# Splitting the first weight matrix out of the key refills of a decode kernel, and reordering its last loads and products

## The chip, the cores and the metric

The kernel runs on one core of a Trainium2 chip. The metric is the device time of one launch in microseconds. The core has a matrix engine (PE, with a separate row PEld for its weight loads), a vector engine (DVE), a scalar engine (ACT), a general engine (POOL) and a sync engine (SP), each with its own instruction stream. They are ordered against each other only by semaphores. Loads from memory are done by 16 DMA engines that work through queues. Nearly all loads of this kernel are issued by SP, so they stand in one queue, in the order in which SP issues them.

## The reference

For two rows `x` of 512 numbers, an attention over a cached window and a two-layer network are computed and mixed by a gate:

```python
q = (x @ wq)                                  # 32 heads of 128, in 8 groups of 4
k = k_cache[:, :, Sk - W:, :]                 # W = 4096 keys for each of 2 x 8 groups
v = v_cache[:, :, Sk - W:, :]
p = softmax(q k^T * Dh ** -0.5)               # 4 heads share one group of keys
a = (p v).reshape(B, Sq, Hq * Dh) @ wo
h = x @ w1 + b1                               # 512 -> 1792
b = (h * tanh(softplus(h))) @ w2              # 1792 -> 512
g = sigmoid((x * gate_w).sum(-1))
out = g * a + (1 - g) * b
```

All numbers are float32. Keys and values of the window are 33.5 MB each, `wq` and `wo` 8.4 MB each, `w1` and `w2` 3.7 MB each. Every byte is used once.

## The kernel before, in words

The work runs in eight turns, one for each group of keys (`HKV`), in a loop on each engine. The last turn differs a little, so several loops have seven passes (`PAIRS`) and a written-out eighth. There is one buffer for keys, `kslot`, and one for values, `vslot`.

`kslot` holds, for each of 128 partitions, 4 KB of `w1` (`w1s`, two of the fourteen 128-column blocks of `w1`), 32 KB of keys (`ks`) and 8 KB of the query weights of the next turn (`wqs`). One load fills it in each turn but the last. `vslot` holds 32 KB of values (`vs`), 4 KB of `w2` (`w2s`) and 8 KB of `wo` (`wos`), both of the turn before. The load of the first turn brings values alone, since nothing stood before it; the load of the seventh is split (values, then the rest: lines 124 and 127). In the last turn keys and values come in three pieces each, and behind them the `w2` and `wo` of the seventh turn and then the `wo` of the eighth (`wol`, three pieces).

What a turn does on each engine:

- **DVE** (`head`, lines 316 to 347) waits for the key load (`ld_k`). It makes the dot products of `x` with the four 512-wide halves of `w1s` (4 instructions, `hx`) and with the next turn's query weights (8 instructions, `queries`, `q8`); all of these stand at line 282. When PE has finished the scores it reduces their maximum (line 322), then writes the next queries into `qz` (line 291, `queries_out`). After the exponential it transposes the probabilities (line 330), forms the reciprocal of their sum and the factor `mkr`, waits for POOL's denominator (`hd`) and inverts it (line 339), waits for PE's product (`sD`), scales and reduces it (lines 342 and 345), and stores the attention output of the turn as weights for PE (`wst`, line 347).
- **PE** makes the scores (line 229) as soon as keys and queries are there, a few small products, the product of probabilities and values (line 240, signal `sD`), the products with `w2` (line 247) and `wo` (line 253) of the turn before, which go into one accumulator `acc` (signal `sP`), and the sum over the parts of the attention output (line 258).
- **ACT** takes the exponentials: that of the activation function (line 210), then that of the scores (line 212).
- **POOL** computes the activation function from `hx` (lines 184 to 201) and hands it to PE as `hst` (signal `hs`), one turn ahead of its use.

The order of the work around the change is set by SP's stream (lines 110 to 139). The key load of a turn waits for `qz` of the turn before, that is for the last use of `kslot` by DVE and PE. The value load waits for `sP` of the turn before (for `sD` alone in turns seven and eight, where only values are overwritten). SP works in order: a load behind a wait is issued when the wait is over.

At the end (lines 260 to 276, `last`) the accumulator is copied to `accs`, folded over its four row blocks by a product with `fold`, and the four blocks of the last `wo` are multiplied with `wst`. Two halves of the partitions of `fin` take these products: the upper half (`s = 1`) first `fold` and blocks 0 and 1, the lower half (`s = 0`) blocks 2 and 3. ACT copies the upper half to `fs` after the first signal `pe` (line 218), DVE adds it to the lower half after the second (line 354), and SP stores the result (line 358).

Of the kernel before, what the change touches and what calls it, by code (L numbers as in the profile page):

```python
# [4 lines left out]
AF = mybir.ActivationFunctionType  # L5
# [3 lines left out]
P = 128  # L9
B = 2  # L10
# [13 lines left out]
PAIRS = FC // 2  # L24
CHUNK = 8192
W1P = 2 * D
WQH = REP * D
SCALE = DH ** -0.5
BIG = 3.0e38
S = 16  # L30
# [2 lines left out]
NP = PAIRS - 1  # L33


def decode_kernel(nc, xg, wq0, kw, k7a, k7b, k7c, v0, vw, v6, ww5, v7a, v7b, v7c, w26, wo6, wo7a, wo7b, wo7c, out):
    T, V, A, G, SP = nc.tensor, nc.vector, nc.scalar, nc.gpsimd, nc.sync

    def sb(name, n, p=P):
        return nc.alloc_sbuf_tensor(name, [p, n], F32).ap()  # L40

    def ps(name, n):
        return nc.alloc_psum_tensor(name, [P, n], F32).ap()

    kslot = sb("kslot", W1P + CHUNK + WQH)
    w1s, ks, wqs = kslot[:, :W1P], kslot[:, W1P : W1P + CHUNK], kslot[:, W1P + CHUNK :]
    vslot = sb("vslot", CHUNK + 2 * D + WQH + S)
    vs, w2s, wos = vslot[:, :CHUNK], vslot[:, CHUNK : CHUNK + 2 * D], vslot[:, CHUNK + 2 * D : CHUNK + 2 * D + WQH]
    b1 = vslot[:, CHUNK + 2 * D + WQH : CHUNK + 2 * D + WQH + FC]
# [5 lines left out]
    b16, qz, wst, hst = (zeros[:, sum(widths[:i]) : sum(widths[: i + 1])] for i in range(len(widths)))  # L55
# [4 lines left out]
    fold = sb("fold", Q)  # L60
# [10 lines left out]
    q8 = sb("q8", B * REP)  # L71
    mx = sb("mx", 1)
    bias = sb("bias", 1)
    prob = sb("prob", 512)
    lsum = sb("lsum", 1)
    pT = sb("pT", 512)
    rcp = sb("rcp", 1)
    mkr = sb("mkr", BN)
    osc = sb("osc", BN * DH)
    osel = sb("osel", DH)  # L80
    junkw = sb("junk", 12 * D + P)
    junk = [junkw[:, j * D : j * D + D] for j in range(12)]
    hx = sb("hx", 4)
    hb = sb("hb", 4)
    pq = sb("pq", 8)
    mt = sb("mt", 4)
    mn = sb("mn", 4)
    md = sb("md", 4)
    mr = sb("mr", 4)
    accs = sb("accs", D)  # L90
    fs = sb("fs", 256, 64)
    res = sb("res", 256, 64)

    acc = ps("acc", D)
    sc = ps("sc", 512)
# [4 lines left out]
    lp = small[:, 0:1]  # L100
    ol = small[:, 8:16]

    names = ("ld_x ld_q ld_k ld_kb ld_kc ld_v ld_vb ld_vc ld_h ld_o ld_w0 ld_w1 ld_w2 c_id c_m c_z c_xb c_eg c_g c_mg "
             "gx g0 g1 g2 g3 g4 g5 hs vx q8 rcp os0 qz mx sA sB bias ex pT sC osel sD sP sE wst pq mkr hx hq hd hr accs pe fs res st").split()
    sem = {n: nc.alloc_semaphore(n) for n in names}


# [5 lines left out]
    for i in range(HKV):  # L113
        if i:
            SP.wait_ge(sem["qz"], S * (i + 1))
        if i < PAIRS:
            SP.dma_start(kslot, kw[i]).then_inc(sem["ld_k"], 16)
        else:
            for n, (f, t), src in zip(("ld_k", "ld_kb", "ld_kc"), parts, (k7a, k7b, k7c)):
                SP.dma_start(ks[:, f:t], src).then_inc(sem[n], 16)  # L120
        if i in (0, NP):
            if i:
                SP.wait_ge(sem["sD"], S * i)
            SP.dma_start(vs, (v0, v6)[i // NP]).then_inc(sem["ld_v"], 16)
            if i:
                SP.wait_ge(sem["sP"], S * i)
                SP.dma_start(vslot[:, CHUNK : CHUNK + 2 * D + WQH], ww5).then_inc(sem["ld_h"], 16)
        elif i < NP:
            SP.wait_ge(sem["sP"], S * i)
            SP.dma_start(vslot[:, : CHUNK + 2 * D + WQH], vw[i - 1]).then_inc(sem["ld_v"], 16)  # L130
        else:
            SP.wait_ge(sem["sD"], S * i)
            for n, (f, t), src in zip(("ld_v", "ld_vb", "ld_vc"), parts, (v7a, v7b, v7c)):
                SP.dma_start(vs[:, f:t], src).then_inc(sem[n], 16)
    SP.wait_ge(sem["sP"], S * PAIRS)
    SP.dma_start(w2s, w26).then_inc(sem["ld_h"], 16)
    SP.dma_start(wos, wo6).then_inc(sem["ld_o"], 16)
    for n, (f, t), src in zip(("ld_w0", "ld_w1", "ld_w2"), ((0, 2), (2, 3), (3, 4)), (wo7a, wo7b, wo7c)):
        SP.dma_start(wol[:, f * D : t * D], src).then_inc(sem[n], 16)
# [24 lines left out]
    for n in range(NH):  # L164
        i = G.tensor_copy(same.rearrange("p (j y n h) -> p j y n h", j=NJ, n=NH, h=REP)[:, :, :, n, :],
                          key.rearrange("p (y h) -> p y h", h=REP)[:, None].to_broadcast([P, NJ, 4, REP]))
# [39 lines left out]
    A.wait_ge(sem["c_eg"], 1)  # L206
    A.activation(eg, zg, AF.Exp, scale=-1.0).then_inc(sem["c_eg"], 1)
    with A.Fori(S, S * PAIRS + 1, S) as r:
        A.wait_ge(sem["pq"], r)
        A.activation(pq, pq, AF.Exp).then_inc(sem["hq"], S)  # L210
        A.wait_ge(sem["bias"], r)
        A.activation(prob, sc, AF.Exp, bias=bias, scale=SCALE, accum_out=lsum).then_inc(sem["ex"], S)  # L212
    A.wait_ge(sem["bias"], S * HKV)
    A.activation(prob, sc, AF.Exp, bias=bias, scale=SCALE, accum_out=lsum).then_inc(sem["ex"], S)
    A.wait_ge(sem["sP"], S * HKV)
# [6 lines left out]
    with T.Fori(S, S * (HKV) + 1, S) as r:  # L222
# [4 lines left out]
        for m in range(BN):  # L227
            for j in range(NJ):
                i = T.matmul(sc[Q * j : Q * j + Q, :], qz[:, m * Q : m * Q + Q],  # L229
                             ks[:, (m * NJ + j) * 512 : (m * NJ + j + 1) * 512],  # L230
                             start=(m == 0), stop=(m == BN - 1))
# [6 lines left out]
        for c in range(NC):  # L238
            j = c % NJ
            i = T.matmul(o[Q * j : Q * j + Q, :], pT[:, c * Q : c * Q + Q], vs[:, c * 512 : c * 512 + 512],  # L240
                         start=(c < NJ), stop=(c >= NC - NJ))
# [4 lines left out]
        for j in range(2):  # L246
            i = T.matmul(acc[Q * j : Q * j + Q, :], hst[:, j * Q : j * Q + Q], w2s[:, j * D : j * D + D],  # L247
                         start=False, stop=False, skip_group_check=True)
# [3 lines left out]
        for j in range(REP):  # L252
            i = T.matmul(acc[Q * j : Q * j + Q, :], wst[:, j * Q : j * Q + Q], wos[:, j * D : j * D + D],  # L253
                         start=False, stop=False, skip_group_check=True)
# [5 lines left out]
    def last(s, lhs, rhs, wait=None, **kw):  # L260
        for u in range(2):
            a = Q * (2 * s + u)
            i = T.matmul(fin[a : a + Q, :256], lhs, rhs[:, u * 256 : u * 256 + 256], skip_group_check=True, **kw)  # L263
            if wait is not None and u == 0:
                i.wait_op(*wait, "sem-ge")
        return i

    def wo(j):
        return wst[:, j * Q : j * Q + Q], wol[:, j * D : j * D + D]

    last(1, fold, accs, (sem["accs"], 1), start=True, stop=False)
    T.wait_ge(sem["wst"], S * (HKV + 1))
    last(1, *wo(0), (sem["ld_w0"], 16), start=False, stop=False)
    last(1, *wo(1), start=False, stop=True).then_inc(sem["pe"], 1)
    last(0, *wo(2), (sem["ld_w1"], 16), start=True, stop=False)
    last(0, *wo(3), (sem["ld_w2"], 16), start=False, stop=True).then_inc(sem["pe"], 1)


    def dots(out, col, lhs, n, first=0):
        for c in range(n):  # L280
            for b in range(B):
                i = V.tensor_tensor_reduce(out=junk[first + c * B + b], in0=lhs[:, c * D : c * D + D], in1=xb[b], op0=ALU.mult,  # L282
                                           op1=ALU.add, scale=1.0, scalar=0.0, accum_out=out[:, col(c, b) : col(c, b) + 1])
        return i
# [22 lines left out]
    for b in range(B):  # L307
        i = V.tensor_tensor_reduce(out=junk[8 + b], in0=xs[:, B * D :], in1=xb[b], op0=ALU.mult, op1=ALU.add, scale=1.0, scalar=0.0,
                                   accum_out=zg[:, b : b + 1])
# [6 lines left out]
    def head(r, more):  # L316
        if more:
            V.wait_ge(sem["ld_k"], r)
            dots(hx, lambda c, b: c * B + b, w1s, 2, 8).then_inc(sem["hx"], S)
            queries(wqs, "q8", S)  # L320
        V.wait_ge(sem["sA"], r)
        V.tensor_reduce(mx, sc, axis=AX.X, op=ALU.max).then_inc(sem["mx"], S)  # L322
        if more:
            V.wait_ge(sem["q8"], r)
            queries_out()
        V.wait_ge(sem["sB"], r)
        V.tensor_tensor_reduce(out=junkw[:, 12 * D :], in0=mb[:, :P], in1=mask, op0=ALU.add, op1=ALU.min, scale=-SCALE,  # L327
                               scalar=BIG, accum_out=bias).then_inc(sem["bias"], S)
        V.wait_ge(sem["ex"], r)
        V.transpose(pT, prob).then_inc(sem["pT"], S)  # L330
        if more:
            V.wait_ge(sem["c_mg"], 1)
        V.wait_ge(sem["sC"], r)
        V.reciprocal(rcp, lp).then_inc(sem["rcp"], S)
        V.wait_ge(sem["rcp"], r)
        V.tensor_scalar_mul(mkr, m4g, rcp).then_inc(sem["mkr"], S)
        if more:
            V.wait_ge(sem["hd"], r)
            V.reciprocal(mr, md).then_inc(sem["hr"], S)  # L339
        V.wait_ge(sem["mkr"], r)  # L340
        V.wait_ge(sem["sD"], r)
        V.tensor_tensor(osc.rearrange("p (m d) -> p m d", m=BN), o.rearrange("p (m d) -> p m d", m=BN),  # L342
                        mkr[:, :, None].to_broadcast([P, BN, DH]), op=ALU.mult).then_inc(sem["os0"], S)
        V.wait_ge(sem["os0"], r)
        V.tensor_reduce(osel, osc.rearrange("p (m d) -> p d m", m=BN), axis=AX.X, op=ALU.add).then_inc(sem["osel"], S)  # L345
        V.wait_ge(sem["sE"], r)
        V.tensor_copy(wstv, ol.rearrange("p (b h) -> p h b", b=B)).then_inc(sem["wst"], S)

# [59 lines left out]
```

## Time and profile before

| | before |
|---|---|
| median of three runs | 223.78 us (223.70 to 224.45) |
| profiled execution: its own time | 223.85 us |
| profiled execution: span of the core | 221.3 us |
| PE busy | 116.1 us (52%) |
| DVE busy | 94.4 us (43%) |
| POOL busy | 38.1 us (17%) |
| ACT busy | 10.1 us (5%) |
| read from memory | 91.26 MB |
| SP's load queue, share of 16 engines | 96.7% |

The span is what the trace covers; the device time has some 2.5 us outside it. Busy time counts instructions on an engine, overlapping ones once. The queue's share is the time that its packets took on the 16 DMA engines, divided by 16 spans.

### The profile page before, as it was taken

To read this page: it belongs to the slowest core of one execution; us is meant where nothing else is said; L and a number is where in the kernel's file an instruction comes from. 1 tells how busy PE (TensorE), PEld (TensorE's weight loads), DVE (VectorE), ACT (ScalarE), POOL (GpSimd) and SP (SyncE) were. 2 spreads that over 40 slices of the span, in tenths; PEclk is the share of its full clock that TensorE was granted. 3 is DMA by queue.
4 is the path that set the end of the run, shared out by engine and by line. 5 is a ranking of instruction groups with operands and counts; after the bars stand their busy time and mean duration, and the time that the engine had idled before them with its cause. 6 is when DMAs were issued, how large, how long until landed. Compare 5 with 4: busy or idle time off the path is not lost.

```text
span 221.3 us, 2097 instructions
## 1 busy us (share of the span) xinstructions
PE 116.1 (52%) x668; PEld 34.0 (15%) x668; DVE 94.4 (43%) x284; ACT 10.1 (5%) x27; POOL 38.1 (17%) x97
## 2 busy tenths in 40 slices
PE   0003769082491916829187441926429183983863
PEld 0001122020120212202121111201112020220201
DVE  1297933097031960329403492026811187131131
ACT  2000010001000010000100001000010001000001
POOL 8000700034000430006100070001600024000000
PEclk9999957859587575876658796785967859698599
DMA  8999999999999999999999999999999898999990
GB/s 314 395 415 457 409 340 423 407 464 432 407 464 432 407 448 440 415 440 440 423 415 464 423 407 472 415 407 480 415 407 480 384 456 383 431 420 428 411 404 28
DMA packets 3977, 91.33 MB, mean 413 GB/s; under 512 B 452, under 2 KB 516, under 8 KB 1032
## 3 DMA queue, kind: packets, MB, share of 16 engines
q1 hardware_dynamic: 3968, 91.30, 96.7%
q10 hardware_dynamic: 8, 0.02, 0.0%
q14 instruction: 1, 0.01, 0.0%
HBM read 91.26 MB, written 0.07 MB: 413 GB/s over the span
## 4 chain that ended last, share of the span: by engine, by line
DMA 66%; DVE 24%; PE 5%; issue 3%; ACT 1%; SPq 0%; ACTq 0%; DVEq 0%
DMA kslot<-in_kw 58%; DVE junk L282 22%; DMA vslot<-in_wo 8%; PE o L240 2%; PE acc L253 1%; PE fin L263 1%; DVE zeros L291 0%; DVE mx L322 0%; DVE q L282 0%; PE acc L247 0%; DVE pT L330 0%; ACT accs L216 0%; DVE res L354 0%; SPq L110 0%; ACT fs L218 0%
## 5 line engine op out<-in xcount | busy, mean ns | idle before, releaser
L229 PE MATMUL sc<-kslot,zeros 128*32 128x512 f32 x256 | 44.8, 857 | 52.1 <-DMA kslot<-in_kw 50.3
L282 DVE CUSTOM_DVE_ANT_0 junk<-kslot,xs 128x512 f32<-128x512 f32 x84 | 52.0, 688 | 28.7 <-DMA kslot<-in_kw 28.7
L240 PE MATMUL o<-vslot,pT 128*32 128x512 f32 x256 | 46.5, 889 | 16.5 <-DMA vslot<-in_vw 15.1
L342 DVE TENSOR_TENSOR osc<-o,mkr 128x512 f32<-128x512 f32 x8 | 5.5, 692 | 58.5 <-PE o L240 58.5
L229 PEld LDWEIGHTS sc<-kslot,zeros 128*32 128x32 f32 x256 | 11.1, 150 | 78.9 <-issue 75.5
L240 PEld LDWEIGHTS o<-vslot,pT 128*32 128x32 f32 x256 | 11.2, 154 | 44.9 <-issue 41.6
L253 PE MATMUL acc<-vslot,zeros 128*32 128x512 f32 x64 | 14.2, 599 | 1.4 <-DMA vslot<-in_wo 1.4
L185 POOL TENSOR_TENSOR hb<-hx,zeros 128x4 f32<-128x4 f32 x7 | 3.4, 488 | 51.1 <-DVE hx L282 51.1
L200 POOL TENSOR_TENSOR zeros<-mn,omg 128x4 f32<-128x4 f32 x7 | 1.4, 201 | 60.0 <-PE acc L253 60.0
L235 PE MATMUL mb<-ident,mx 128*128 128x128 f32 x8 | 2.5, 313 | 16.8 <-DVE mx L322 16.8
L236 PE MATMUL small<-lsum,same 128*128 128x1 f32 x16 | 3.8, 310 | 11.7 <-ACT prob L212 10.2
L330 DVE STREAM_TRANSPOSE pT<-prob 128x512 f32<-128x512 f32 x8 | 5.7, 711 | 7.8 <-ACT prob L212 6.8
L345 DVE TENSOR_REDUCE osel<-osc 128x128 f32<-128x512 f32 x8 | 8.3, 1035 | 0.8
L247 PE MATMUL acc<-vslot,zeros 128*32 128x512 f32 x32 | 8.3, 593 | 0.3 <-DMA vslot<-in_w 0.3
L322 DVE TENSOR_REDUCE mx<-sc 128x1 f32<-128x512 f32 x8 | 5.5, 688 | 5.7 <-PE sc L229 5.7
L210 ACT ACTIVATE pq<-pq 128x8 f32<-128x8 f32 x7 | 1.5, 209 | 132.4 <-POOL pq L189 132.4
L212 ACT ACTIVATE prob<-sc,bias 128x512 f32<-128x512 f32 x7 | 4.8, 687 | 29.8 <-DVE bias L327 29.8
L191 POOL TENSOR_TENSOR mt<-pq 128x4 f32<-128x4 f32 x7 | 5.1, 735 | 3.2 <-ACT pq L210 3.2
L197 POOL TENSOR_TENSOR mn<-mn,mr 128x4 f32<-128x4 f32 x7 | 1.4, 199 | 24.4 <-DVE mr L339 24.4
L236 PEld LDWEIGHTS small<-lsum,same 128*128 128x128 f32 x16 | 3.4, 265 | 13.1 <-issue 13.1
L282 DVE DVE_READ_ACCUMULATOR2_ANT q<- 128x1 f32 x64 | 5.3, 82 | 0.0
L282 DVE CUSTOM_DVE_ANT_0 junk<-vslot,xs 128x512 f32<-128x512 f32 x8 | 5.0, 685 | 0.0
(61 smaller groups left out, 63.7 us busy)
## 6 DMA issues: line engine op xcount, KB each, us to landing
kslot<-in_kw SPq DMA_DIRECT2D x7, 5632.0 KB, 18.5
vslot<-in_vw SPq DMA_DIRECT2D x5, 5632.0 KB, 18.8
vslot<-in_v SPq DMA_DIRECT2D x2, 4096.0 KB, 22.6
kslot<-in_k7a SPq DMA_DIRECT2D x1, 2048.0 KB, 10.1
vslot<-in_v7a SPq DMA_DIRECT2D x1, 2048.0 KB, 12.1
vslot<-in_ww SPq DMA_DIRECT2D x1, 1536.0 KB, 19.3
vslot<-in_wq SPq DMA_DIRECT2D x1, 1031.0 KB, 5.5
kslot<-in_k7b SPq DMA_DIRECT2D x1, 1024.0 KB, 12.2
```

Of the source, the lines that this page charges most:

```text
L191: then(G.tensor_tensor(mt, pq[:, 4:], pq[:, 4:], op=ALU.add), "g1")
L212: A.activation(prob, sc, AF.Exp, bias=bias, scale=SCALE, accum_out=lsum).then_inc(sem["ex"], S)
L229: i = T.matmul(sc[Q * j : Q * j + Q, :], qz[:, m * Q : m * Q + Q], ks[:, (m * NJ + j) * 512 : (m * NJ + j + 1) * 512], start=(m == 0), sto ...
L236: after(T.matmul(lp, same, lsum, start=True, stop=True), "ex").then_inc(sem["sC"], S)
L240: i = T.matmul(o[Q * j : Q * j + Q, :], pT[:, c * Q : c * Q + Q], vs[:, c * 512 : c * 512 + 512], start=(c < NJ), stop=(c >= NC - NJ))
L247: i = T.matmul(acc[Q * j : Q * j + Q, :], hst[:, j * Q : j * Q + Q], w2s[:, j * D : j * D + D], start=False, stop=False, skip_group_check= ...
L253: i = T.matmul(acc[Q * j : Q * j + Q, :], wst[:, j * Q : j * Q + Q], wos[:, j * D : j * D + D], start=False, stop=False, skip_group_check= ...
L282: i = V.tensor_tensor_reduce(out=junk[first + c * B + b], in0=lhs[:, c * D : c * D + D], in1=xb[b], op0=ALU.mult, op1=ALU.add, scale=1.0, ...
L322: V.tensor_reduce(mx, sc, axis=AX.X, op=ALU.max).then_inc(sem["mx"], S)
L330: V.transpose(pT, prob).then_inc(sem["pT"], S)
L342: V.tensor_tensor(osc.rearrange("p (m d) -> p m d", m=BN), o.rearrange("p (m d) -> p m d", m=BN), mkr[:, :, None].to_broadcast([P, BN, DH] ...
L345: V.tensor_reduce(osel, osc.rearrange("p (m d) -> p d m", m=BN), axis=AX.X, op=ALU.add).then_inc(sem["osel"], S)
```

## The change

- All of `w1` gets a buffer of its own (`w1s`, 28 KB a partition) and is loaded once, behind the first value load. The seven key loads are 4 KB a partition shorter.
- In each of the first seven turns DVE copies that turn's 4 KB from `w1s` to a fixed place (`w1c`), with a start address from a register, and the four dot products read the copy. They stand behind the transpose of the probabilities instead of ahead of the queries.
- The inversion of POOL's denominator moves behind the reduction at line 345. ACT takes the exponential of the scores ahead of that of the activation function.
- In the last turn the `w2` of the seventh turn is loaded ahead of the values, and both wait for `sP`; the values waited for `sD` before.
- At the end the upper half takes blocks 0 and 1 of `wo` alone, and the folding of the accumulator goes to the lower half, ahead of blocks 2 and 3.

```diff
-    kslot = sb("kslot", W1P + CHUNK + WQH)
-    w1s, ks, wqs = kslot[:, :W1P], kslot[:, W1P : W1P + CHUNK], kslot[:, W1P + CHUNK :]
+    kslot = sb("kslot", CHUNK + WQH)
+    ks, wqs = kslot[:, :CHUNK], kslot[:, CHUNK:]
+    w1s = sb("w1s", PAIRS * W1P)
+    w1c = sb("w1c", W1P)
...
             if i:
                 SP.wait_ge(sem["sP"], S * i)
                 SP.dma_start(vslot[:, CHUNK : CHUNK + 2 * D + WQH], ww5).then_inc(sem["ld_h"], 16)
+            else:
+                SP.dma_start(w1s, w1).then_inc(sem["ld_w"], 16)
...
         else:
-            SP.wait_ge(sem["sD"], S * i)
+            SP.wait_ge(sem["sP"], S * i)
+            SP.dma_start(w2s, w26).then_inc(sem["ld_h"], 16)
             for n, (f, t), src in zip(("ld_v", "ld_vb", "ld_vc"), parts, (v7a, v7b, v7c)):
                 SP.dma_start(vs[:, f:t], src).then_inc(sem[n], 16)
-    SP.wait_ge(sem["sP"], S * PAIRS)
-    SP.dma_start(w2s, w26).then_inc(sem["ld_h"], 16)
...
     with A.Fori(S, S * PAIRS + 1, S) as r:
+        A.wait_ge(sem["bias"], r)
+        A.activation(prob, sc, AF.Exp, bias=bias, scale=SCALE, accum_out=lsum).then_inc(sem["ex"], S)
         A.wait_ge(sem["pq"], r)
         A.activation(pq, pq, AF.Exp).then_inc(sem["hq"], S)
-        A.wait_ge(sem["bias"], r)
-        A.activation(prob, sc, AF.Exp, bias=bias, scale=SCALE, accum_out=lsum).then_inc(sem["ex"], S)
...
-    last(1, fold, accs, (sem["accs"], 1), start=True, stop=False)
     T.wait_ge(sem["wst"], S * (HKV + 1))
-    last(1, *wo(0), (sem["ld_w0"], 16), start=False, stop=False)
+    last(1, *wo(0), (sem["ld_w0"], 16), start=True, stop=False)
     last(1, *wo(1), start=False, stop=True).then_inc(sem["pe"], 1)
-    last(0, *wo(2), (sem["ld_w1"], 16), start=True, stop=False)
+    last(0, fold, accs, (sem["accs"], 1), start=True, stop=False)
+    last(0, *wo(2), (sem["ld_w1"], 16), start=False, stop=False)
     last(0, *wo(3), (sem["ld_w2"], 16), start=False, stop=True).then_inc(sem["pe"], 1)
...
             V.wait_ge(sem["ld_k"], r)
-            dots(hx, lambda c, b: c * B + b, w1s, 2, 8).then_inc(sem["hx"], S)
             queries(wqs, "q8", S)
...
         V.transpose(pT, prob).then_inc(sem["pT"], S)
         if more:
+            V.wait_ge(sem["ld_w"], 16)
+            V.tensor_copy(w1c, w1s[:, bass.ds((r - S) * (W1P // S), W1P)]).then_inc(sem["w1c"], S)
+            V.wait_ge(sem["w1c"], r)
+            dots(hx, lambda c, b: c * B + b, w1c, 2, 8).then_inc(sem["hx"], S)
             V.wait_ge(sem["c_mg"], 1)
...
-        if more:
-            V.wait_ge(sem["hd"], r)
-            V.reciprocal(mr, md).then_inc(sem["hr"], S)
...
         V.tensor_reduce(osel, osc.rearrange("p (m d) -> p d m", m=BN), axis=AX.X, op=ALU.add).then_inc(sem["osel"], S)
+        if more:
+            V.wait_ge(sem["hd"], r)
+            V.reciprocal(mr, md).then_inc(sem["hr"], S)
```

More of the change, by code (lines that the diff above doesn't have):

```diff
@@ L33, with decode_kernel @@
 NP = PAIRS - 1
-def decode_kernel(nc, xg, wq0, kw, k7a, k7b, k7c, v0, vw, v6, ww5, v7a, v7b, v7c, w26, wo6, wo7a, wo7b, wo7c, out):
+def decode_kernel(nc, xg, wq0, w1, kw, k7a, k7b, k7c, v0, vw, v6, ww5, v7a, v7b, v7c, w26, wo6, wo7a, wo7b, wo7c, out):
     T, V, A, G, SP = nc.tensor, nc.vector, nc.scalar, nc.gpsimd, nc.sync
@@ L101, in decode_kernel @@
     ol = small[:, 8:16]
-    names = ("ld_x ld_q ld_k ld_kb ld_kc ld_v ld_vb ld_vc ld_h ld_o ld_w0 ld_w1 ld_w2 c_id c_m c_z c_xb c_eg c_g c_mg "
-             "gx g0 g1 g2 g3 g4 g5 hs vx q8 rcp os0 qz mx sA sB bias ex pT sC osel sD sP sE wst pq mkr hx hq hd hr accs pe fs res st").split()
+    names = ("ld_x ld_q ld_k ld_kb ld_kc ld_v ld_vb ld_vc ld_w ld_h ld_o ld_w0 ld_w1 ld_w2 c_id c_m c_z c_xb c_eg c_g c_mg "
+             "gx g0 g1 g2 g3 g4 g5 hs vx q8 rcp os0 qz mx sA sB bias ex pT sC osel sD sP sE wst pq mkr w1c hx hq hd hr accs pe fs res st").split()
     sem = {n: nc.alloc_semaphore(n) for n in names}
@@ L388 @@
         "wq0": np.concatenate([wq[0], b1], axis=1),
-        "kw": np.concatenate([w1, k[:PAIRS], wq[1:]], axis=2),
+        "w1": w1.transpose(1, 0, 2).reshape(P, PAIRS * W1P),
+        "kw": np.concatenate([k[:PAIRS], wq[1:]], axis=2),
         "k7a": k[PAIRS, :, : 2 * h], "k7b": k[PAIRS, :, 2 * h : 3 * h], "k7c": k[PAIRS, :, 3 * h :],
```

## The prediction

> **What bounds the kernel now.** I read the page first: its span, its DMA line, its queue and its chain.
>
> ```profile
> span 221.3 us, 2097 instructions
> DMA  8999999999999999999999999999999898999990
> q1 hardware_dynamic: 3968, 91.30, 96.7%
> DMA kslot<-in_kw 58%; DVE junk L282 22%; DMA vslot<-in_wo 8%; PE o L240 2%; PE acc L253 1%; PE fin L263 1%; DVE zeros L291 0%; DVE mx L322 0%; DVE q L282 0%; PE acc L247 0%; DVE pT L330 0%; ACT accs L216 0%; DVE res L354 0%; SPq L110 0%; ACT fs L218 0%
> ```
>
> The DMA engines are busy in all slices but the last, and one queue accounts for 96.7% of them. The chain puts 22% on DVE's dot products, though, between key loads. Whether those cost anything depends on whether the queue ran empty behind them. So next come the chain in order of time, whose key pieces give issue and landing, and the list of loads.
>
> ```profile
> 1.17 18.72 DMA kslot<-in_kw
> ...
> 28.07 16.66 DMA kslot<-in_kw
> ...
> 159.52 18.48 DMA kslot<-in_kw
> ```
> ```profile
> kslot<-in_kw SPq DMA_DIRECT2D x7, 5632.0 KB, 18.5
> vslot<-in_vw SPq DMA_DIRECT2D x5, 5632.0 KB, 18.8
> vslot<-in_v SPq DMA_DIRECT2D x2, 4096.0 KB, 22.6
> ```
>
> Start plus length is the landing: K0 at 19.89, K1 at 44.73, K6, five loads later, at 178.00. From K1 to K6 a turn takes 133.27 / 5 = 26.65 us and moves one key and one value load, 2 x 5632 KB = 11.53 MB: **432.8 GB/s**, with no room left behind the dot products. Only the first step is slower. Between K0 and K1 the queue moves 4096 + 5632 KB = 9.96 MB, 23.02 us at that rate, but it takes 24.84. The missing **1.8 us** can be seen in windows of a quarter microsecond (the last two columns are the DMA engines' share and what the packets that start there carry, in GB/s):
>
> ```profile
> 28.50:28.75 0.25, 0.00 (x0) 0.00 (x0) 0.21 (x1) 0.00 (x0) 0.00 (x0) 1.00 0.00 0
> 28.75:29.00 0.25, 0.00 (x0) 0.00 (x0) 0.09 (x2) 0.06 (x1) 0.00 (x0) 0.50 0.00 0
> 29.00:29.25 0.25, 0.00 (x0) 0.00 (x0) 0.00 (x0) 0.25 (x1) 0.00 (x0) 0.50 7.21 2163
> ```
>
> No packet starts from 28.50 to 29.00; then twelve start at once, 540 KB, and each takes 7.21 x 16 x 0.25 / 12 = 2.40 us, where a steady engine (432.8 / 16 GB/s) takes 1.67 us for its 45 KB. K1 was issued at 28.07, when V0 was nearly through (landing 19.89 + 4.19 MB / 432.8 = 29.58). A lead of 1.51 us of the issue before the landing ahead of it was too short.
>
> So the kernel is one stream of loads with a single hole in turn 0, and a tail behind its last byte.
>
> **The change, part by part.**
>
> *w1 out of the key load, behind V0.* The bytes stay the same. K0 is 512 KB shorter, so it lands 0.524 MB / 432.8 = 1.21 us earlier, at 18.68. V0 lands at 28.37 and w1 (3.67 MB, 8.48 us) at 36.85. K1 is needed only then. Its issue waits for turn 0's head:
>
> ```profile
> 18.96 0.17 DVE L314 RECIPROCAL g<-eg 128x2 f32<-128x2 f32 x1
> ...
> 20.03 6.25 PE L229 MATMUL sc<-kslot,zeros 128*32 128x512 f32 x32 [20.03 <-DMA kslot<-in_kw]
> ...
> 27.27 0.69 DVE L322 TENSOR_REDUCE mx<-sc 128x1 f32<-128x512 f32 x1
> ```
>
> Without the four `hx` products (0.61 us apart, 2.45 us) the maximum no longer waits for DVE, but for the scores, which end at 26.28 against 27.27 now: 0.99 us, not 2.45, come out. DVE is free at 19.13, late for K0 by 0.45, and eight products from there end at 24.1, still ahead of the scores (18.68 + 0.14 + 6.25 = 25.07). K1 is issued at 28.07 - 1.21 - 0.99 = 25.87, 11 us ahead of w1's landing. The hole closes: **-1.8 us**. Bounds: 1.27 (if the slowness of the twelve first packets, 0.73 us each or 0.55 a DMA engine, belongs to the load and not to the empty queue) to 1.82; I take 1.8, since the key loads of the later turns, issued into a full queue, show no such loss.
>
> In later turns the key issue comes about 1 us earlier, which gives nothing: those keys already wait in the queue.
>
> *The copy and the products behind the transpose.* The trace has no copy of this size. From below stands the reduction of half as many numbers, 0.69 us (line 322 above); from above the shuffle of as many, 1.28, which I take, to be safe. With the products 1.28 + 2.53 = 3.8 us a turn, seven times, under this cover:
>
> ```profile
> L298 DVE STREAM_SHUFFLE xs<-xs 128x1024 f32<-128x1024 f32 x1 | 1.3, 1282 | 0.0
> ```
> ```profile
> 54.65 0.71 DVE L330 STREAM_TRANSPOSE pT<-prob 128x512 f32<-128x512 f32 x1 [0.98 <-ACT prob L212]
> ...
> 64.29 0.69 DVE L342 TENSOR_TENSOR osc<-o,mkr 128x512 f32<-128x512 f32 x1 [8.46 <-PE o L240]
> ...
> 65.90 0.33 SPq L130 DMA_DIRECT2D vslot<-in_vw  x1
> ```
>
> Between the transpose (ended 55.36) and the scaling (64.29) DVE has half a microsecond of small work, so 3.8 us fit with 4.5 us to spare, and the value load's issue at 65.90 hangs on PE alone. If that cover were gone, osel, `wst` and the next scores would move, not the loads. POOL needs 5.1 us from its first step on `hx` to its denominator, 5.3 with the signal ahead:
>
> ```profile
> 22.64 0.48 POOL L185 TENSOR_TENSOR hb<-hx,zeros 128x4 f32<-128x4 f32 x1 [2.97 <-DVE hx L282]
> ...
> 27.55 0.20 POOL L195 TENSOR_TENSOR md<-mn,mt 128x4 f32<-128x4 f32 x1
> ```
>
> With `hx` at about 59 the inversion finds it ready at 64 to 65, ahead of its new place (osel ends at 66.1). Turn 0 is the tight one: the new wait for w1 stands on DVE at 36.85, and behind it the rest of the head, PE's sum (line 258) and with it the next scores. Copy and products end at 40.7, POOL at 46.0, `wst` at 46.5; K1 lands at 36.85 + 5.24 MB / 432.8 = 48.96. That leaves 2.5 us: 0. ACT's other order: the activation exponential has always waited longer than the scores': 0.
>
> *Value loads against shorter key loads.* This is the price of the shorter keys. A value load issues when PE is done with the value load before it, and must be in the queue before the key load ahead of it runs out:
>
> ```profile
> 92.89 0.33 SPq L130 DMA_DIRECT2D vslot<-in_vw  x1
> ...
> 119.87 0.33 SPq L130 DMA_DIRECT2D vslot<-in_vw  x1
> ...
> 145.15 0.33 SPq L130 DMA_DIRECT2D vslot<-in_vw  x1
> ```
>
> With the issue at 65.90 above these are the loads V2 to V5 (V1, ahead of whose key load w1 now stands, only gains). Against key landings every 26.65 us from 44.73, at 71.38, 98.03, 124.69 and 151.34, the leads are 5.48, 5.14, **4.82** and 6.19 us, and no turn lost time. Keys shorter by 1.21 us make them 4.27, 3.93, **3.61** and 4.98. The needed lead lies between 1.51 (lost 1.8) and 4.82 (lost nothing). If lateness is paid one for one, it is 1.51 + 1.8 = 3.3; the need is made of the issue's way to the first packet, about 0.95 us in the hole, and of the spread between the first and the last DMA engine to run dry. I take 3.3, the hole being the only row in which a lead was too short, so 0; the other end, 4.82, costs 0.55 + 0.89 + 1.21 = 2.65 us.
>
> [...]
>
> *w2 ahead of the last values, both behind `sP`.* That wait ended at 195.81 where `sD` ended at 194.10:
>
> ```profile
> 194.10 0.33 SPq L134 DMA_DIRECT2D vslot<-in_v7a  x1
> ...
> 195.81 0.33 SPq L136 DMA_DIRECT2D vslot<-in_w  x1
> ...
> 201.31 1.07 PE L229 MATMUL sc<-kslot,zeros 128*32 128x512 f32 x8 [1.41 <-DMA kslot<-in_k7c]
> ```
>
> Queued behind it on SP are `w26`, all of V7, `wo6` and the last `wo`. The key piece ahead of them landed by 201.3: a lead of 5.5 us, above every bound: 0. The bytes ahead of `wo6` are the same, so it lands as before; V7 lands 1.21 us later. What follows V7:
>
> ```profile
> 213.21 1.03 DVE L345 TENSOR_REDUCE osel<-osc 128x128 f32<-128x512 f32 x1
> ...
> 215.03 1.06 PE L253 MATMUL acc<-vslot,zeros 128*32 128x512 f32 x8 [1.43 <-DMA vslot<-in_wo]
> ...
> 216.03 0.39 PE L258 MATMUL small<-same,osel 128*128 128x8 f32 x2
> ...
> 216.79 0.63 PE L263 MATMUL fin<-accs,fold 128*32 128x256 f32 x4 [0.38 <-ACT accs L216]
> ...
> 217.25 1.07 PE L263 MATMUL fin<-wol,zeros 128*32 128x256 f32 x16
> ...
> 218.33 0.37 ACT L218 COPY fs<-fin 64x256 f32<-64x256 f32 x1 [1.59 <-PE fin L263]
> 218.73 0.42 DVE L354 TENSOR_TENSOR res<-fin,fs 64x256 f32<-64x256 f32 x1 [2.04 <-ACT fs L218]
> ```
>
> osel would end at 214.24 + 1.21 = 215.45, and line 258, which reads it, stands behind `wo6`'s products at 216.03. It holds by 0.6 us: 0.
>
> *The closing products.* Now all products end at 218.32, then ACT's copy takes 0.37, then DVE adds. After, the upper half has two products instead of three, so its copy starts about 0.5 us earlier (217.8) and ends at 218.2, under the lower half. That half now has three products in place of two and starts no later; I let it end where PE ends now, or 0.1 later. DVE starts at 218.4 instead of 218.73: **-0.3 us**. Bounds: 0 (the third product adds its 0.4) to 0.41 (the whole step from PE's end to DVE's start).
>
> Sum: -1.8 - 0.3 = **-2.1 us** on the profiled 223.85, that is 221.75; the runs' median is 0.07 below that execution: **221.7 us**.
>
> **The rivals.**
>
> *The tail meets a slow clock* (about the same time). The closing stretch ran at the full granted clock, the start of the last value product did not:
>
> ```profile
> 206.00:208.00 2.00, 1.70 (x9) 0.47 (x13) 0.32 (x2) 0.00 (x0) 0.00 (x0) 0.50 0.98 410
> ...
> 210.00:212.00 2.00, 1.54 (x16) 0.16 (x8) 0.00 (x0) 0.00 (x0) 0.00 (x0) 1.00 1.05 428
> ```
> ```profile
> L240 PE MATMUL o<-vslot,pT x256: 592/1057/1064, 30.6 to 211.7; 128*32 128x512 f32 x128
> ```
>
> V7 lands 1.21 us later, so PE starts that product later after its pause. If the clock has not come up by `wo6`'s landing, its products (1.06 us) and the closing ones (1.53) take 1057 / 592 = 1.79 times as long: +2.0, giving 223.7. For it: each pause of PE is followed by a stretch at 0.50. Against: V7's products are then packed closer to the tail, which should raise the clock in time. [...] I give this rival 9%.
>
> *Value loads come too late* (slower). Its place is the queue at the end of each key load in turns 1 to 4. It decides when the needed lead exceeds 3.61 us, and eats the whole gain at about 4.6. At 4.82 the sum is 221.7 + 2.65 = 224.4; if besides PE works every value load off as late as in the worst turn (lead 3.6 in all four), the loss is 4 x 1.2 = 4.9 and the time 226.6. For it: three of the four leads fall below any that the trace shows without loss. Against: the hole prices the need at 3.3. I put it at 225 when it comes; 9%, about half of it above 0.5%.
>
> *The hole is not closed* (the change does not do what it says): the 1.8 us are a cost of the stream's start that comes up again elsewhere, say when K1 follows w1. Only the tail's 0.3 remains: 223.4. Against: half a microsecond without any packet right after a late issue. 6%.
>
> *The chain is taken at its word* (much faster): four products of 0.61 us leave seven turns, 17 us, giving 206. Against: 91.3 MB at 432.8 GB/s alone are 211 us. 3%.
>
> **How the numbers follow.** The forecast has 70%, the rivals 27%, and 3% is left for something slower that I do not see. The bound between a change and none is 0.5%, 222.66 and 224.90. The forecast's own range is 221.3 (hole 1.82, tail 0.41, and the spread of the runs) to 222.5 (1.27 and 0). Downwards I go to 221.2; upwards to 223.5, which takes in the unclosed hole, a tail with part of its slow clock and a mild lateness of the values. Faster: forecast and chain, 0.71 after the few per cent of it that end above 222.66; same: the slow tail, the unclosed hole, half of the late values and that rest, 0.21; slower 0.08.
>
> **What would show it.** Right: K0 lands near 18.7, K1 is issued near 26 and the windows behind it hold packets throughout; `w1` lands near 36.9; key landings in turns 2 to 6 are 25.44 us apart (11.01 MB at 432.8); the last add on DVE follows PE directly, not ACT. Wrong: key landings more than 25.5 apart with windows free of packets just before a value load's first packets (late values); granted clock 0.50 at the closing products (slow tail); a hole behind w1; DVE still at its products when K1 lands.

## The result, and the profile after

The changed kernel took 222.12 us in the median of 20 runs, beside 223.50 for the kernel before in as many runs: a ratio of **0.9934** (95% interval 0.9910 to 0.9959), 1.4 us between the medians. The ratios leave out executions over 1.5% above the fastest of their kernel, which the medians and ranges keep. Two repetitions beside new runs of the kernel before gave 0.9923 (0.9888 to 0.9958) and 0.9924 (0.9891 to 0.9958), with medians of 221.67 and 222.28 us. So it is faster, by about 0.7%, where 0.94% was forecast (2.1 of 223.78 us).

The execution profiled with the first result took 224.96 us, far above its median; the lines of "after" below are those of a later execution of the same kernel, at 221.64 us (span 220.1, against 221.3 in 223.85 before). The page of that one, beside which the page of before showed 96.7% for the queue and 38.1 us of POOL:

```profile
span 220.1 us, 2112 instructions
PE 115.0 (52%) x668; PEld 35.1 (16%) x668; DVE 99.6 (45%) x291; ACT 10.1 (5%) x27; POOL 21.2 (10%) x97
DMA  8899999999999999999999999999999999999991
q1 hardware_dynamic: 4112, 91.30, 97.2%
```

The queue's share is up from 96.7 to 97.2% of a shorter span, and POOL's work has nearly halved (more on that at the end). The next lines are PE's timeline after: the scores of a turn start some 0.13 us after the key load has landed (the chain has K1 issued at 24.87 and landed 24.05 us later, at 48.92), so the first number, less 0.13, is the key landing.

```profile
18.70 5.24 PE L232 MATMUL sc<-kslot,zeros 128*32 128x512 f32 x32 [18.70 <-DMA kslot<-in_kw]
...
49.05 5.42 PE L232 MATMUL sc<-kslot,zeros 128*32 128x512 f32 x32 [5.82 <-DMA kslot<-in_kw]
...
74.52 6.33 PE L232 MATMUL sc<-kslot,zeros 128*32 128x512 f32 x32 [4.06 <-DMA kslot<-in_kw]
...
99.96 5.34 PE L232 MATMUL sc<-kslot,zeros 128*32 128x512 f32 x32 [3.12 <-DMA kslot<-in_kw]
...
125.95 6.22 PE L232 MATMUL sc<-kslot,zeros 128*32 128x512 f32 x32 [4.17 <-DMA kslot<-in_kw]
...
151.41 5.34 PE L232 MATMUL sc<-kslot,zeros 128*32 128x512 f32 x32 [3.25 <-DMA kslot<-in_kw]
...
177.18 6.20 PE L232 MATMUL sc<-kslot,zeros 128*32 128x512 f32 x32 [4.18 <-DMA kslot<-in_kw]
```

From SP's queue after, the issue of K1 and of the values V2 to V5, and from DVE the first copy, which waits for `w1`:

```profile
24.87 0.33 SPq L119 DMA_DIRECT2D kslot<-in_kw  x1
...
69.74 0.33 SPq L134 DMA_DIRECT2D vslot<-in_vw  x1
...
96.11 0.33 SPq L134 DMA_DIRECT2D vslot<-in_vw  x1
...
121.06 0.33 SPq L134 DMA_DIRECT2D vslot<-in_vw  x1
...
147.43 0.33 SPq L134 DMA_DIRECT2D vslot<-in_vw  x1
```
```profile
36.93 0.69 DVE L335 COPY w1c<-w1s 128x1024 f32 x1 [9.59 <-DMA w1s<-in_w]
```

**The hole is gone.** K1 is issued at 24.87, `w1` is there for the copy at 36.93, and K1 for the scores 12.12 us later, which is what its 5.24 MB take at 432.8 GB/s (12.11). From K0 to K1 it is 30.35 us where the bytes of V0, `w1` and K1 take 30.28. So the added load shows no cost of its own.

**A smaller loss has come in.** Key landings after that should be 25.44 us apart. They are 25.47, 25.44, **25.99**, 25.46 and **25.77**. The value load between two key landings was issued ahead of the first of them by (landing, that is scores' start less 0.13, minus issue):

| value load | lead, us | next key landing above 25.44, us |
|---|---|---|
| V2 | 74.39 - 69.74 = 4.65 | 0.00 |
| V3 | 99.83 - 96.11 = 3.72 | 0.55 |
| V4 | 125.82 - 121.06 = 4.76 | 0.02 |
| V5 | 151.28 - 147.43 = 3.85 | 0.33 |

The two short leads are the two late turns: 0.9 us of the 2.1 forecast are lost there in this execution.

**The tail** after, in order of time:

```profile
213.52 1.05 DVE L348 TENSOR_REDUCE osel<-osc 128x128 f32<-128x512 f32 x1
...
214.08 1.07 PE L256 MATMUL acc<-vslot,zeros 128*32 128x512 f32 x8 [0.67 <-DMA vslot<-in_wo]
215.07 0.39 PE L261 MATMUL small<-same,osel 128*128 128x8 f32 x2
215.20 0.58 ACT L219 COPY accs<-acc 128x512 f32<-128x512 f32 x1 [11.16 <-PE acc L256]
...
216.98 0.37 ACT L221 COPY fs<-fin 64x256 f32<-64x256 f32 x1 [1.19 <-PE fin L266]
217.51 0.42 DVE L360 TENSOR_TENSOR res<-fin,fs 64x256 f32<-64x256 f32 x1 [1.78 <-PE fin L266]
```

ACT's copy of the upper half (216.98) ends ahead of PE now, and DVE's last sum waits for PE. From the start of the accumulator's copy to the start of that sum it is 217.51 - 215.20 = 2.31 us; before it was 218.73 - 216.16 = 2.57.

### The profile page after: what moved, and what is told of

It reads as the page before. It is cut to its first block, busy times and chain, and to the rows that moved or that the text cites. A ratio compares the mean times of both kernels' runs of the same rounds, so it can differ in the third digit from the quotient of the medians.

```text
span 223.6 us, 2112 instructions
## 1 busy us (share of the span) xinstructions
PE 112.6 (50%) x668; PEld 33.7 (15%) x668; DVE 99.7 (45%) x291; ACT 10.1 (5%) x27; POOL 21.4 (10%) x97
## 4 chain that ended last, share of the span: by engine, by line
DMA 72%; PE 24%; SPq 1%; issue 1%; DVE 0%; DVEq 0%
DMA vslot<-in_vw 45%; DMA vslot<-in_v 19%; PE o L243 18%; DMA vslot<-in_wo 8%; PE acc L256 3%; PE acc L250 2%; PE fin L266 1%; SPq L139 1%; SPq L119 0%; DVE res L360 0%; SPq L112 0%; PE small L261 0%; SPq L137 0%; DVE zeros L353 0%; DVEq L359 0%
## 5 line engine op out<-in xcount | busy, mean ns | idle before, releaser
L232 PE MATMUL sc<-kslot,zeros 128*32 128x512 f32 x256 | 42.6, 818 | 46.9 <-DMA kslot<-in_kw 44.2
L243 PE MATMUL o<-vslot,pT 128*32 128x512 f32 x256 | 45.6, 874 | 30.1 <-DMA vslot<-in_vw 25.8
L285 DVE CUSTOM_DVE_ANT_0 junk<-kslot,xs 128x512 f32<-128x512 f32 x56 | 34.9, 688 | 22.5 <-DMA kslot<-in_kw 22.4
L345 DVE TENSOR_TENSOR osc<-o,mkr 128x512 f32<-128x512 f32 x8 | 5.5, 692 | 46.6 <-PE o L243 46.5
L285 DVE CUSTOM_DVE_ANT_0 junk<-w1c,xs 128x512 f32<-128x512 f32 x28 | 17.7, 688 | 0.2
L188 POOL TENSOR_TENSOR hb<-hx,zeros 128x4 f32<-128x4 f32 x7 | 1.4, 201 | 114.0 <-DVE hx L285 114.0
L335 DVE COPY w1c<-w1s 128x1024 f32 x7 | 4.6, 657 | 9.8 <-DMA w1s<-in_w 9.8
L261 PE MATMUL small<-same,osel 128*128 128x8 f32 x16 | 3.1, 267 | 9.9 <-DVE osel L348 9.9
L261 PEld LDWEIGHTS small<-same,osel 128*128 128x128 f32 x16 | 2.6, 203 | 16.9 <-issue 16.9
```

The source lines that it names most:

```text
L261: after(T.matmul(ol, osel, key_rhs, start=True, stop=True), "osel").then_inc(sem["sE"], S)
L335: V.tensor_copy(w1c, w1s[:, bass.ds((r - S) * (W1P // S), W1P)]).then_inc(sem["w1c"], S)
```

## The experiments

Two theories stood against each other for what was missing. Theory A: the shorter keys make value loads late. Rival B: one DMA engine lags from the start, and no hole lets the others wait for it. The experiments ran in three groups; the kernels of one group ran on the same chip beside the same runs of the kernel before. The changed kernel stands in the first and third group, the first version with two places in the second.

### The changed kernel again

> The changed kernel once more. Forecast as on record: 2.1 us under the kernel before (ratio 0.991). Theory A (value loads issue too late, in turns 1 to 4): the hole in turn 0 is closed (1.8 us) and the tail is shorter (0.3), but the value loads whose issue comes less than some 3 us ahead of the first DMA engine that needs them begin with packets of over 1.8 us instead of 1.67, and key to key landings of those turns are 0.5 to 1.5 above 25.44; net gain 0.5 to 1.6 us, changing with the phase of the granted clock. Rival B (a DMA engine lags from the start, since without the hole nothing lets the others wait for it): landings 25.44 apart in all turns, but first and last engine over 1.8 us apart from K0 on, where they were 1.3 to 1.4 before; net gain about 1.5.

Measured: 0.9923 (0.9888 to 0.9958), 1.9 us between the medians. Its profile is the one above. The short leads and the late turns fall together, as Theory A has it; Rival B's evenly spaced landings are not there. Nor is its lag: each load raises its semaphore 16 times, read here as once for each DMA engine, and the first and last of K0's sixteen times in the kept trace are 1.18 us apart, where Rival B wanted over 1.8. In the execution at 224.96 us, though, they are 1.88 apart and K0's scores start at 19.47 instead of 18.70, so a lag from the start exists too, in that execution.

### Values and weights loaded apart

```diff
-            SP.wait_ge(sem["sP"], S * i)
-            SP.dma_start(vslot[:, : CHUNK + 2 * D + WQH], vw[i - 1]).then_inc(sem["ld_v"], 16)
+            SP.wait_ge(sem["sD"], S * i)
+            SP.dma_start(vs, vm[i - 1]).then_inc(sem["ld_v"], 16)
+            SP.wait_ge(sem["sP"], S * i)
+            SP.dma_start(vslot[:, CHUNK : CHUNK + 2 * D + WQH], wm[i - 1]).then_inc(sem["ld_h"], 16)
```

> The changed kernel with the value load of turns 1 to 5 split: 4096 KB of values behind the signal of the value product (sD), then 1536 KB of w2 and wo behind sP, as the seventh turn has it already. The values issue about 1.7 us earlier, the queue's order and bytes stay. Theory A: no slow first packets any more, key to key landings 25.44 in every turn from K2 to K6, time 2.0 us or more under the kernel before, and 0.5 to 1 under the changed kernel, with less spread from run to run. Rival B: nothing gained against the changed kernel (within 0.2 us), since the values were never late.

Measured: 0.9928 (0.9899 to 0.9958), median 221.94 us, all twelve runs between 221.62 and 222.32; the changed kernel beside it went from 221.26 to 223.28. First and last of the five turns on PE:

```profile
49.26 6.41 PE L228 MATMUL sc<-kslot,zeros 128*32 128x512 f32 x32 [5.81 <-DMA kslot<-in_kw]
...
176.91 5.74 PE L228 MATMUL sc<-kslot,zeros 128*32 128x512 f32 x32 [8.05 <-DMA kslot<-in_kw]
```

The landings are (176.91 - 49.26) / 5 = 25.53 us apart, and evenly so. The late turns are gone, which speaks for Theory A, but the median did not fall: 0.09 us a turn go to the loads in two pieces, 0.45 in five turns, so the test gives with one hand what it takes with the other, and the 0.5 to 1 us that Theory A expected did not come. A cleaner version was needed.

### Two places for w2 and wo

The value buffer gets a second place for `w2` and `wo` on its other side. Odd turns fill that and the values, even turns the values and the old place, each in one load, and the load waits for `sD` only. PE's loop has two turns in its body.

```diff
-            SP.wait_ge(sem["sP"], S * i)
-            SP.dma_start(vslot[:, : CHUNK + 2 * D + WQH], vw[i - 1]).then_inc(sem["ld_v"], 16)
+            SP.wait_ge(sem["sD"], S * i)
+            SP.dma_start(vall[:, : WW + CHUNK] if i % 2 else vslot[:, : CHUNK + WW], vw[i - 1]).then_inc(sem["ld_v"], 16)
```

> The changed kernel with two places for w2 and wo, one on each side of the values in the value buffer, used in turn by odd and even turns. A value load of turns 1 to 5 is still one transfer of 5632 KB, but it overwrites nothing that the products with w2 and wo still read, so it waits for sD instead of sP: 1.7 us earlier, no load added. Theory A: no slow first packets, key to key landings 25.44 from K1 to K6 (25.53 where the loads were split), last landing 0.7 to 0.9 ahead of the changed kernel's, time 2.0 to 2.8 us under the kernel before, spread of the runs under 1 us. Rival B (a lagging engine): as the changed kernel, within 0.2 us.

Measured: 0.9918 (0.9892 to 0.9944), median 221.22 us, six runs between 221.09 and 221.71. By its ratio it is no faster than the changed kernel in the first group (0.9923). It was run again beside the changed kernel:

> The changed kernel again, as the measure for the other three on the same chip. Theory A (late values): 1.4 to 1.8 us under the kernel before, wider spread than the version with two places; in its profile the key landings that follow a lead under 4 us lie 0.3 to 1.5 above 25.45, the others do not.

> The changed kernel with two places for w2 and wo, again, now beside the changed kernel. Theory A: 0.3 to 0.9 us under the changed kernel in the median, all runs within 1 us; 2.1 us under the kernel before. Rival B (a lagging engine alone): equal to the changed kernel within 0.2.

Measured: the changed kernel 222.28 us (0.9924, 0.9891 to 0.9958; 221.10 to 225.73), the two places **221.06** (0.9884, 0.9839 to 0.9929; 221.03 to 221.45). PE's timeline of the second one:

```profile
49.40 5.93 PE L239 MATMUL sc<-kslot,zeros 128*32 128x512 f32 x32 [5.82 <-DMA kslot<-in_kw]
...
176.73 5.34 PE L239 MATMUL sc<-kslot,zeros 128*32 128x512 f32 x32 [3.27 <-DMA kslot<-in_kw]
```

The landings are 127.33 / 5 = 25.47 us apart. With the value loads out of the way the median falls by 1.2 us in this group. The intervals of the two ratios overlap, but five of the six executions lie under ten of the changed kernel's eleven. This is the fastest version of the study, by its median.

The changed kernel's trace of this group bears Theory A out only in part. Of its two leads under 4 us, 3.89 is followed by a landing 0.46 late, as expected, and 3.95 by one 0.02 late, which was not expected.

### The two places in the kernel before

The same two places, with `w1` in the key loads and the old closing order.

> The kernel before with the same two places and the value loads behind sD; w1 in the key loads, the hole and the old closing order stay. Its leads become 6.5 to 8 us. Theory A: the kernel before loses little to late values in most executions (at most 0.3 in the median), but its slower executions go; median 0 to 0.6 us under the kernel before, the hole of 1.8 us stays between V0 and K1. The difference to the two places with w1 out is then the hole and the tail alone: 2.1 us by the prediction's step.

> The kernel before with the two places, again. With the values out of the way the difference between this and the changed kernel with two places is the hole and the tail alone: 2.1 us by the prediction's steps (1.8 + 0.3); 0.3 if the hole's loss came up again elsewhere.

Measured: 1.0020 (0.9992 to 1.0049) and 0.9994 (0.9961 to 1.0027), medians 223.28 and 223.25 us. No change: in the kernel before, the values were early enough. Theory A also expected the slower executions to go, and they did not (up to 225.37 and 224.46 us): the spread of the kernel before has another source. The first key landings of the first execution, on PE:

```profile
20.05 5.41 PE L236 MATMUL sc<-kslot,zeros 128*32 128x512 f32 x32 [20.05 <-DMA kslot<-in_kw]
...
44.89 4.94 PE L236 MATMUL sc<-kslot,zeros 128*32 128x512 f32 x32 [6.53 <-DMA kslot<-in_kw]
...
71.83 5.12 PE L236 MATMUL sc<-kslot,zeros 128*32 128x512 f32 x32 [5.88 <-DMA kslot<-in_kw]
```

The first step is 24.84 us, that of before, so the hole stays when only the values are early. In the trace of the repetition it is longer:

```profile
20.27 5.49 PE L236 MATMUL sc<-kslot,zeros 128*32 128x512 f32 x32 [20.27 <-DMA kslot<-in_kw]
...
45.62 6.46 PE L236 MATMUL sc<-kslot,zeros 128*32 128x512 f32 x32 [6.96 <-DMA kslot<-in_kw]
```

That is 25.35 us, a hole of 2.3. The difference between the two pairs, with and without the change, is 223.28 - 221.22 = 2.06 and 223.25 - 221.06 = 2.19 us in the medians. **This agrees with the forecast's 2.1 us**, measured with the late values taken out of both sides. It does not settle the size to tenths: the ratios differ by 0.0102 and 0.0110, that is 2.3 and 2.5 us, and their intervals leave about 1 us either way (an estimate from the intervals).

### Values later still

The reverse dose: the value loads wait for `wst` too, in both kernels.

```diff
             SP.wait_ge(sem["sP"], S * i)
+            SP.wait_ge(sem["wst"], S * (i + 1))
             SP.dma_start(vslot[:, : CHUNK + 2 * D + WQH], vw[i - 1]).then_inc(sem["ld_v"], 16)
```

In the kernel before:

> The kernel before with the value loads of turns 1 to 5 waiting also for the store of the attention output (wst), 1.0 us after sP; nothing else changed. Leads against the key landings become 5.2 (V1), 4.5, 4.1, 3.8 and 5.2 us instead of 6.2, 5.5, 5.1, 4.8 and 6.2. The prediction's price (need 3.3 us): no change. Theory A (need near 4.8): the loads V3 and V4 begin with slow packets and land 0.7 to 1.2 us late each, V2 up to 0.5; time 1 to 2.5 us above the kernel before.

Measured: 1.0016 (0.9978 to 1.0054), no change that can be told. SP's queue and PE's scores in its execution:

```profile
121.54 0.33 SPq L131 DMA_DIRECT2D vslot<-in_vw  x1
...
148.51 0.33 SPq L131 DMA_DIRECT2D vslot<-in_vw  x1
```
```profile
126.23 5.95 PE L230 MATMUL sc<-kslot,zeros 128*32 128x512 f32 x32 [5.03 <-DMA kslot<-in_kw]
...
152.87 6.28 PE L230 MATMUL sc<-kslot,zeros 128*32 128x512 f32 x32 [4.71 <-DMA kslot<-in_kw]
...
179.72 6.51 PE L230 MATMUL sc<-kslot,zeros 128*32 128x512 f32 x32 [4.48 <-DMA kslot<-in_kw]
```

A lead of 126.10 - 121.54 = 4.56 us is followed by a step of 26.64, nothing lost (26.65 is the rate); one of 152.74 - 148.51 = 4.23 by 26.85, 0.2 lost. Theory A in the form "need near 4.8" expected 1 to 2.5 us and was too high. In the changed kernel:

> The changed kernel with the value loads of turns 1 to 5 waiting for the store of the attention output (wst) besides sP. In turns 1 to 5 the issue is 0.9 us later than sP, more where the denominator's inversion stands ahead of it. Leads against the key landings fall to 2.7 to 4 us. Theory A: nearly every engine begins these loads with a slow packet or runs dry, 0.8 to 1.5 us lost in each of four turns: 3 to 6 us above the changed kernel. The prediction's price (need 3.3, paid one for one): at most 0.6 in a turn, 0 to 1.5 in all.

Measured: 1.0053 (1.0026 to 1.0080), median 224.56 us, that is 2.3 to 2.9 us above the changed kernel's medians in the other two groups. More than the prediction's price (0 to 1.5), a little less than Theory A's 3 to 6. These are the turns of V2 to V5 in all the kept traces, sorted by lead (value loads in one piece):

| lead, us | next key landing late by, us, one number for each turn |
|---|---|
| 4.56 and more | none over 0.03 |
| 4.08 to 4.23 | 0.05, 0.14, 0.20 |
| 3.85 to 3.97 | 0.02, 0.24, 0.33, 0.46, 1.21 |
| 3.63 to 3.72 | 0.55, 0.59, 1.52 |
| 3.18 to 3.49 | 1.26, 2.12, 2.42 |

The 1.21 and 1.52 are from the execution at 224.96 us, the last row from one of this version at 227.16 us, both far above their medians. So the loss starts near 4 us and grows below, but the lead alone does not fix its size. And one kind of loss has nothing to do with the lead. The version with the old last order, below, is 0.48 us late from K1 to K2, with V1 issued 16.8 us ahead:

```profile
49.23 5.90 PE L240 MATMUL sc<-kslot,zeros 128*32 128x512 f32 x32 [5.81 <-DMA kslot<-in_kw]
...
75.15 6.59 PE L240 MATMUL sc<-kslot,zeros 128*32 128x512 f32 x32 [3.79 <-DMA kslot<-in_kw]
```

The same step is 0.26 and 0.29 late in the two profiled executions with two places of the second group, and 0.19 in the kernel before with later values (lead 6.3). No figure here shows whether a part of the DMA engines fell behind there, as Rival B has it; the cause is open.

### A warm PE

```diff
+        for c in range(24):
+            j = c % NJ
+            T.matmul(fin[Q * j : Q * j + Q, :], same[:, :Q], xs[:, :512], start=True, stop=True, skip_group_check=True)
         T.wait_ge(sem["ld_v"], r)
```

> The changed kernel with 24 more products in each turn on PE, between the sum of the exponentials and the wait for the values, into a bank that nothing reads before the end; they do nothing for the result. They fill PE's pause, so that the value product starts at the full granted clock: 0.43 instead of 0.86 us a pass over the four groups. Theory A with the clock as what makes the values late: from a value landing to the next value issue 6 us instead of 7.2 to 8.5, so leads of 5 us or more, no slow first packets, landings 25.44 apart, time 0.5 to 0.9 under the changed kernel. If the clock isn't the cause: no fewer slow packets; if the extra products stand in the way: up to 2 us slower.

Measured: 1.0060 (1.0026 to 1.0094), median 224.88 us, slower. PE and SP in turn 1 and turn 4:

```profile
59.25 6.76 PE L242 MATMUL fin<-xs,same 128*32 128x512 f32 x48
65.84 3.61 PE L246 MATMUL o<-vslot,pT 128*32 128x512 f32 x32
...
71.23 0.33 SPq L134 DMA_DIRECT2D vslot<-in_vw  x1
...
136.41 4.03 PE L242 MATMUL fin<-xs,same 128*32 128x512 f32 x33
140.25 3.62 PE L246 MATMUL o<-vslot,pT 128*32 128x512 f32 x32
...
145.65 0.33 SPq L134 DMA_DIRECT2D vslot<-in_vw  x1
```

The value product now takes 3.6 us instead of 5.3 to 6.5, and the granted clock is 0.87 in the mean of the execution instead of 0.775. In turn 4 the extra products were through when the values came, and the issue came 5.4 us after the product's start: a lead of 6.4 us, and no late landing. In turn 1 they ran 6.76 us and held the product until 65.84, and in the last turn they lay in the tail. The leads of V2 to V4 stayed at 3.7 to 4.1 us. So the clock does move the lead, but the test paid more than it won, and as a proof that the clock alone makes the leads short it is inconclusive.

### The closing products alone, and the order of the last loads

> The kernel before with the new order of the closing products alone (upper half blocks 0 and 1, lower half fold, blocks 2 and 3). The prediction's step: DVE's last sum starts 0.3 us closer to the landing of the last wo piece, time 0.3 us less (bounds 0 to 0.41). Rival: the third product on the lower half takes it all back: 0.

Measured: 0.9997 (0.9960 to 1.0035). A third of a microsecond is below what this interval can tell. The profile shows the step itself, ACT's copy of the accumulator and DVE's last sum:

```profile
216.63 0.59 ACT L216 COPY accs<-acc 128x512 f32<-128x512 f32 x1 [11.19 <-PE acc L253]
...
218.95 0.42 DVE L354 TENSOR_TENSOR res<-fin,fs 64x256 f32<-64x256 f32 x1 [1.78 <-PE fin L263]
```

2.32 us against 2.57 before: -0.25, in a kernel where nothing else was changed.

The version with two places, but with the values of the last turn behind `sD` again and `w26` behind them:

> The changed kernel with two places, but with the last turn's loads in the old order: values behind sD, then the seventh turn's w2 behind sP. The closing products keep their new order. The prediction priced the order of these loads at 0: no difference to the two places with the new order, within 0.2 us; the values land 1.2 us earlier and osel with them, but wo's landing and the products behind it stand where they stood. Rival: the earlier values let the tail start sooner, up to 0.6 us less; or the order was worth something that the two-place version loses here, up to 0.5 more.

Measured: 221.29 us, 0.9903 (0.9873 to 0.9933), against 221.06 and 0.9884 (0.9839 to 0.9929) with the new order: no difference that can be told, as priced. Three of its eleven executions are 222.3 us or more, so two places do not keep every execution fast.

## Why the prediction was right, and where it was not

**The hole: right.** K0 landed at 18.6 (18.68 expected), `w1` by 36.9 (36.85), K1 at 48.9 (48.96). K1's issue came at 24.87 instead of 25.87, since the scores of turn 0 took 5.24 us and not 6.25; it did not matter, with 11 us to spare. The size of 1.8 came from a single execution. In the four others with the hole that were profiled it was 1.8 and 2.3 (two places in the kernel before), 2.2 (closing products alone) and 2.7 (later values):

```profile
20.34 5.99 PE L230 MATMUL sc<-kslot,zeros 128*32 128x512 f32 x32 [20.34 <-DMA kslot<-in_kw]
...
46.08 5.08 PE L230 MATMUL sc<-kslot,zeros 128*32 128x512 f32 x32 [6.82 <-DMA kslot<-in_kw]
```

That step is 25.74 us where the bytes need 23.02. So the term of 1.8 is the smallest of five, and three of them lie above its upper bound of 1.82.

**Copy and products behind the transpose: right, with more room than thought** (read from the trace; no run takes this part alone, nor ACT's other order or the moved inversion). The copy takes 0.66 us, just under the lower of its two bounds. Turn 0 was expected to be through at 46.5; POOL's chain took half its former time, and `wst` is stored earlier than that:

```profile
43.33 0.17 DVE L353 COPY zeros<-small 128x8 f32<-128x8 f32 x1
```

**Value loads against shorter keys: this step failed**, in its size. It said that the needed lead was 3.3 us, worked out from the hole as if lateness were paid one for one, and took 0. The mechanism and its place, turns 1 to 4, were named as a rival, and the bounds of 1.51 and 4.82 us hold, but the need is about 4: leads of 3.72 and 3.85 cost 0.55 and 0.33 us, leads of 4.65 and more nothing. Nor were the leads the 4.27, 3.93, 3.61 and 4.98 of the prediction: they change with the value product, which took 5.46 to 6.50 us in the turns before them. The loss is 0.9 us in the profiled execution, 0.5 in the third group's and 2.7 in the one at 224.96 us. So it is one source of the spread of the changed kernel (220.87 to 224.96 in the first result); the version with two places, which lifts every lead, stayed within 0.6 us in its two sets of six. The hole was a poor yardstick: there no packet started for half a microsecond and twelve then started at once, and its loss is not one for one with the lead.

**w2 ahead of the last values: right.** osel ended at 214.57, 0.5 us ahead of the end of the products that stand before its reader (0.6 expected), and going back to the old order, in the version with two places, changed nothing that can be told.

**The closing products: right**, -0.25 to -0.26 against -0.3; the lower half's third product costs 0.05 us more than assumed.

**The sum.** -1.8 - 0.26 + 0.9 gives -1.2, and the spans of the two profiled executions differ by 1.2 us. With the late values removed from both kernels it is 2.06 to 2.19 against 2.1. That the forecast of 221.7 lies so near the medians has luck in it. The execution it starts from has a short span, 221.3 us, where those of the three groups have medians of 221.7 to 222.2, partly since its hole was small; and it has 2.5 us outside the span, where 1.3 to 1.4 is usual. The two nearly cancel. And a hole larger than 1.8 pays for part of the late values.

Of the rivals, the late values came, in that execution at about a third of their priced 2.65 us, so they ate part of the gain and not all. The unclosed hole and the chain taken at its word fell. The tail met no slow clock: `wo6`'s products took 1.07 us as before (1.06), and the granted clock was 1.00 from 210 us on. One of the prediction's signs does not serve: quarter microseconds in which no packet starts are found in a full queue too (thirteen of fifty from 25 to 37.5 us in the execution at 224.96 us, three times two in a row).

## What to carry to other kernels

In this kernel, bound by one queue of loads (96.7% of 16 engines' span before, 97.2% after), the chain of waits showed the waits of whoever consumes the loads, and most of them were free (22% of it stood on DVE's dot products before, and the only loss between loads was the hole's 1.8 us); what counted was each issue's lead over the landing ahead of it. Here leads of 4.6 us and more cost nothing for V2 to V5, and those under 4 nearly always something. Before bytes are moved from one load to another, list the leads of all loads that follow the shorter one, and do not take the threshold from a case where the queue ran empty altogether: take it as unknown up to the smallest lead that was seen to be free. A buffer whose parts come free at different times can be laid out so that the next load waits for the first part alone, which gave back here what the shorter keys had cost.

## What was not expected of the hardware

**POOL ran twice as fast.** Its share fell from 38.1 to 21.2 us with the same 97 instructions. The same line before and after, each seven times:

```profile
L194 POOL TENSOR_TENSOR mn<-mn,pq 128x4 f32<-128x4 f32 x7 | 4.6, 656 | 0.0
```
```profile
L197 POOL TENSOR_TENSOR mn<-mn,pq 128x4 f32<-128x4 f32 x7 | 1.4, 199 | 0.0
```

Before, POOL's chain ran beside DVE's dot products (from 22.64 on in turn 0, where DVE was at line 282); after, it runs when these are done. The next step of the chain before, of the same size, comes when DVE has gone on to the maximum (27.55 in turn 0), and is as fast as after:

```profile
L195 POOL TENSOR_TENSOR md<-mn,mt 128x4 f32<-128x4 f32 x7 | 1.4, 199 | 1.0
```

So the traces have 656 ns for a step of this size beside DVE's dot products and 199 away from them. No run here isolates why.

**A late load started slowly, even into a queue that was not empty.** Two windows over the first packets of V5, of the changed kernel and of the two places (the last two numbers are DMA share and GB/s):

```profile
149.00:150.00 1.00, 0.00 (x0) 0.00 (x0) 0.00 (x0) 0.00 (x0) 0.00 (x0) 1.00 1.50 578
```
```profile
149.00:150.00 1.00, 0.00 (x0) 0.00 (x0) 0.00 (x0) 0.00 (x0) 0.00 (x0) 0.82 1.66 713
```

The same DMA engines spend 1.50 on 578 GB/s in the one and 1.66 on 713 in the other: 11% more time for a byte when the load was issued 3.85 us ahead. The slow start was there at a longer lead too, without a late landing (0.02 us): over the first packets of V4 (123.5 to 125.0, lead 4.76) the changed kernel spends 1.16 on 475 GB/s, the two places 1.10, that is 5% more. Why the first packets of these loads were slow was not settled.
